# Handing out weight conversions and token sums by summed work, after the attention

## The chip, the core and the metric

The kernel runs on one core of one Trainium2 chip. The metric is the time of one execution on the device, in microseconds (us). A core has TensorE (PE in the rows, with PEld for its weight loads), VectorE (DVE), ScalarE (ACT), GpSimd (POOL) and the DMA queue of SyncE (SP). Each engine works through its own instructions in the order in which the program lists them; an instruction that waits holds up everything behind it on that engine.

## What is computed

An attention with a window of 32 and a few global tokens, over 4 batches, 8 heads and 544 tokens each, then two gated feed-forward blocks over the 2176 tokens that come out of it.

```python
def _attn_ref(q_l, k_l, v_l, q_g, k_g, v_g):
    ...
    mask = np.abs(pos[:, None] - pos[None, :]) <= window
    s_ll = np.where(mask, s_ll, -1000000000.0)
    s_l = np.concatenate([s_lg, s_ll], axis=-1)
    out_l = np.matmul(sm(s_l), np.concatenate([v_g, v_l], axis=2))
    ...
def _moe_ref(x, w_gate, w_val, w_out, rms_g):
    xn = x / rms * rms_g
    g = xn @ w_gate
    return ((g * (1.0 / (1.0 + np.exp(-g)))) * (xn @ w_val) @ w_out)
def _moe2_ref(x, w_gate, w_val, w_out):
    return ((1.0 / (1.0 + np.exp(-(x @ w_gate)))) * (x @ w_val) @ w_out)
```

The model width is 512, the inner width 1536. The weights come in as 64-bit floats and have to be made into 32-bit ones on the chip.

## The kernel before

**Tokens.** The attention works on 16 tiles of 128 local tokens and a 17th tile that holds the global tokens of all batches. Its work is cut into small steps (`st_k`, `st_q`, `st_sg`, `st_a1` and so on), which `slot` lines up in the order of the list `ORDER` (L1070). `st_a1` (L795) writes the window's masks into PSUM by eight small matmuls (L809, 32 rows by 32 columns each) and adds the scores by 64 more (L816). The tokens that come out are held as two 16-bit parts, `xhi` and `xlo`.

**Feed-forward.** The inner width of the two feed-forward stages is cut into 12 blocks g of 256. Blocks 0 to 2 are done plainly: for a unit of up to 384 tokens, `gv_mm` (L303) makes gate and value for j = 0 and j = 1 in 48 matmuls, `gv_post` (L322) puts the gate on (a `t` on ACT and DVE, then `hhi` on ACT and `hlo` on POOL), and `flush` (L1171) sends out the unit before by `out1` (L488, 24 matmuls, which read `hhi` and `hlo`). `flush` stands between j = 0 and j = 1. Blocks 3 to 5 and 7 to 11 are done by `quad_gv` (L385) on a third of the tokens at a time: 84 matmuls (L364) on sums and differences of the weights (`wc`, made from `sm`) and of the tokens (`tt`, made from `xb` or `ya`), which save multiplications. DVE adds up the products from PSUM into `G` and `V` (L421) and multiplies them (L397); ACT and POOL (L401) make `h` from that. PSUM has four pairs for these products. Block 6 is plain again (`plain_gv`), and `out2` writes the sums of the second stage.

**Attention and feed-forward overlap.** `first` (L1097) lists the units of blocks 0 and 1 that are run beside the attention; a unit needs its tokens. `tick` is called after every few matmuls; it runs so many attention steps that the tokens of the coming units are in time (`due`).

**Side work.** Two lists hold work for DVE, ACT and POOL that TensorE doesn't need at once. `w_jobs` has the weight conversions: a DMA into `raw` (three buffers), ACT's scaling of the high word (L139), DVE's shift (L151), sign (L154) and low bits (L157), then the sums `sm` (L249 to L255) and the splitting into `wgv`, `wc` or `wo` (L187 on ACT, L190 on DVE). `jobs` has the token sums: `x_combos` (L616, L590, L596, L599) and, for the second stage, `y_combos` (L627, L630, L590). `tick` (L1116) takes one item of `jobs` every second or third call and one of `w_jobs` every second to fourth (`pace`), whatever DVE has still to do; an item can be as much as three or five DVE instructions. `w_need` and `j_need` run what is left when TensorE comes to need it.

```python
    def tick(n):
        pace[0] += 1
        if jobs and pace[0] % pace[2] == 0:
            i = min(range(len(jobs)), key=lambda i: (jobs[i][0][1], i))
            jobs.pop(i)[1]()
        if pace[0] % pace[1] == 0:
            w_step()
```

Of the kernel before, what the change touches and what calls it, by code (L numbers as in the profile page):

```python
# [1 line left out]

# [17 lines left out]
def tile_attention_moe_moe(  # L20
# [17 lines left out]
    nc = tc.nc  # L38
# [85 lines left out]
    ES = [nc.vector if c == "d" else nc.gpsimd for c in "ppdd"]  # L124
# [20 lines left out]
    def w_bits(n, j, k):  # L145

        u = w_f[n].bitcast(I32)
        js = range(2) if j is None else [j]
        if k == 0:
            v = u if j is None else u[:, j]  # L150
            nc.vector.tensor_scalar(out=v, in0=v, scalar1=3, scalar2=None, op0=ALU.logical_shift_left)  # L151
        for j in js:
            if k == 0:
                nc.vector.scalar_tensor_tensor(out=u[:, j], in0=w_words[n][j][:, :, 1], scalar=-0x80000000, in1=u[:, j],  # L154
                                               op0=ALU.bitwise_and, op1=ALU.bitwise_or)
            else:
                nc.vector.scalar_tensor_tensor(out=u[:, j], in0=w_words[n][j][:, :, 0], scalar=29, in1=u[:, j],  # L157
                                               op0=ALU.logical_shift_right, op1=ALU.bitwise_or)

    def w_conv1(n):  # L160
        w_ahead(2 * n + (3 if wide else 2))
        w_scale(n)
        w_scale(n)
        if wide:
            w_bits(n, None, 0)

    def w_conv2(n):
        if wide:
            w_bits(n, None, 1)
            w_words.pop(n)  # L170
            w_ahead(2 * n + 5)
            w_scale(n + 1)

    def w_half(n, j):
        w_ahead(2 * n + (j + 3 if wide else 2))
        if wide:
            if len(w_words.get(n, [])) <= j:
                w_scale(n)
            w_bits(n, j, 0)
            w_bits(n, j, 1)  # L180
            w_scale(n + j)
            w_ahead(2 * n + j + 4)
            if j == 1:
                w_words.pop(n)

# [7 lines left out]
    w_jobs = []  # L193
    w_late = []
    w_done = {}

    def w_block(g):
# [5 lines left out]
        jobs = []  # L203

        def small(f):

            def f2():
                f()
                w_step()
            return f2  # L210
# [5 lines left out]
        def conv(w):  # L216
            n = 3 * g + w
            if g < GS:
                return [lambda: (late(), w_half(n, 0)), lambda: w_half(n, 1)]
            return [lambda: (late(), w_conv1(n)), lambda: w_conv2(n)]  # L220

        def plain(w, dst):
            def f():
# [4 lines left out]
                w_scale(3 * g + w + 1)  # L228
            return f

        if g < GS:
# [3 lines left out]
            jobs.append(small(alloc))  # L235
            for w in range(2):
                jobs += conv(w) + [plain(w, lambda w=w: [w_t[g][0][:, :, w, a] for a in range(2)])]
        else:
# [3 lines left out]
            jobs.append(small(alloc))  # L242
            box = {}

            def sums(w):
                x = w_f[3 * g + w].rearrange("p j (a f) -> p (j a) f", a=2)
                sm = pb[1].tile([128, 3, 256], F32, tag="sm", name="sm")
                box[w] = x, sm
                ES[0].tensor_tensor(out=sm[:, 0], in0=x[:, 0], in1=x[:, 2], op=ALU.subtract)  # L249
                ES[1].tensor_tensor(out=x[:, 2], in0=x[:, 2], in1=x[:, 3], op=ALU.add)  # L250

            def sums2(w):
                x, sm = box[w]
                ES[2].tensor_tensor(out=sm[:, 1], in0=x[:, 2], in1=x[:, 0], op=ALU.subtract)
                ES[3].tensor_tensor(out=sm[:, 2], in0=x[:, 1], in1=sm[:, 1], op=ALU.subtract)  # L255

# [9 lines left out]
            for w in range(2):  # L266
                jobs += conv(w)
                if g == GP:
                    def parts(w=w):
                        return [w_t[g][0][:, w, a, 0:4].rearrange("p (j a) f -> p j (a f)", j=2) for a in range(2)]  # L270
                    jobs.append(plain(w, parts))
# [992 lines left out]
```

## Time and profile before

| | us |
|---|---|
| median of 3 runs (lowest, highest) | 930.08 (929.59, 931.49) |
| the profiled execution | 930.12 |
| its span, from the first instruction to the last | 928.3 |
| PE busy, of the span | 884.2 (95%) |
| DVE busy | 644.8 (69%) |
| ACT busy | 373.9 (40%) |
| POOL busy | 298.3 (32%) |

The sum is made against the profiled execution: 930.12 us, of which 1.8 us lie outside the span; it is within 0.1 us of the median. Matmuls overlap, so a full PE says only that it had something to do. Where it is not full, or where its granted clock is under 1.00, time is lost that another order may give back. The attention ends near 250 us; blocks 0 to 2 take until 364 us, and what follows belongs to blocks 3 to 11.

### The profile page before, as it was taken

Reading aid. Unit: us, or ns where it says so; the run is one execution under the profiler, and the core shown is the slowest. Engines: PE = TensorE matmul, PEld = TensorE weight load, DVE = VectorE, ACT = ScalarE, POOL = GpSimd, SP = SyncE. Lnnn points to the kernel's source line nnn. Section 1 sums busy time; section 2 is a strip of 40 time slices with the busy share of each in tenths; the row PEclk is TensorE's granted clock in tenths of the full one; section 3 lists DMA queues with packets and bytes.
Section 4 is the critical chain, followed back from the end, with each engine's and each line's share of the span. In section 5 each row is a group of like instructions: output and inputs, shape, how many; then the busy total and the mean of one; then the engine's idle time right before and its main releaser. Section 6 shows DMA issues by size and latency. Waiting matters only on the chain.

```text
span 928.3 us, 19289 instructions
## 1 busy us (share of the span) xinstructions
PE 884.2 (95%) x8119; PEld 549.8 (59%) x8119; DVE 644.8 (69%) x907; ACT 373.9 (40%) x713; POOL 298.3 (32%) x344
## 2 busy tenths in 40 slices
PE   7678889999997999999999799999999999999998
PEld 4556566666674667666666466656556555556553
DVE  2967676446477787899957977738598566997352
ACT  3766666354453342343423444434344223423120
POOL 5544424223256661223221453242122203112120
PEclk9879999999997999999999999999999999999999
DMA  9987874331012111211201211101122011200102
GB/s 193 233 181 153 174 180 99 74 72 25 4 47 90 47 46 46 91 46 46 92 1 46 86 51 46 46 1 47 46 90 92 1 46 46 91 24 1 68 23 102
DMA packets 94183, 67.19 MB, mean 72 GB/s; under 512 B 59280, under 2 KB 84368, under 8 KB 94096
## 3 DMA queue, kind: packets, MB, share of 16 engines
q1 hardware_dynamic: 94096, 65.95, 26.8%
q8 instruction: 64, 1.05, 0.5%
q14 instruction: 23, 0.19, 0.1%
HBM read 52.17 MB, written 4.46 MB: 61 GB/s over the span
## 4 chain that ended last, share of the span: by engine, by line
PE 82%; DVE 10%; issue 3%; ACT 2%; DMA 1%; POOL 1%; SPq 1%; DVEq 0%; POOLq 0%; ACTq 0%
PE p L364 29%; PE p L521 13%; PE b L311 13%; PE p L499 7%; PE b L499 6%; PE p L462 5%; PE b L747 3%; PE b L816 2%; DVE wf L154 2%; PE b L871 2%; DVE wf L157 1%; DVE wf L151 1%; DVE G L421 1%; PE b L789 1%; DMA raw<-in_moe_w_gate_dram 1%
## 5 line engine op out<-in xcount | busy, mean ns | idle before, releaser
L364 PEld LDWEIGHTS <-wc 128*128 128x128 f16 x2016 | 197.4, 98 | 121.1 <-DVE G L421 4.8
L364 PE MATMUL p<-tt,wc 128*128 128x384 f16 (+1 forms) x1152 | 202.0, 319 | 5.9 <-DVE G L421 5.4
L364 PE MATMUL p<-xhi,wc 128*128 128x384 f16 (+1 forms) x576 | 156.3, 317 | 0.0
L401 POOL TENSOR_TENSOR h<-V,h 128x768 f16<-128x768 f32 (+1 forms) x48 | 80.4, 1696 | 235.5 <-ACT h L398 218.3
L311 PE MATMUL b<-xhi,wgv 128*128 128x384 f16 (+1 forms) x576 | 143.0, 319 | 0.0
L521 PE MATMUL p<-wo,h 128*128 128x512 f16 x612 | 133.4, 379 | 0.0
L499 PEld LDWEIGHTS <-wo 128*128 128x128 f16 x864 | 85.2, 99 | 58.4 <-issue 10.9
L311 PEld LDWEIGHTS <-wgv 128*128 128x128 f16 x864 | 83.2, 98 | 45.8 <-issue 1.9
L521 PEld LDWEIGHTS <-h 128*128 128x128 f16 x612 | 59.8, 98 | 71.1 <-POOL h L401 0.2
L311 PE MATMUL b<-xlo,wgv 128*128 128x384 f16 (+1 forms) x288 | 91.6, 318 | 0.4 <-DVE xlo L921 0.4
L364 PE MATMUL p<-xlo,wc 128*128 128x384 f16 (+1 forms) x288 | 91.4, 317 | 0.0
L481 DVE SCALAR_TENSOR_TENSOR ya<-p,ya 128x768 f32<-128x768 f32 (+3 forms) x42 | 42.3, 1017 | 60.6 <-PE p L521 48.2
L499 PE MATMUL b<-hhi,wo 128*128 128x384 f16 (+1 forms) x288 | 76.0, 330 | 7.4 <-ACT hhi L342 4.9
L428 ACT ACTIVATE sa<-p 128x384 f32<-128x384 f32 (+1 forms) x48 | 22.5, 469 | 132.7 <-PE p L364 119.9
L343 POOL TENSOR_TENSOR hlo<-t,hhi 128x384 f16<-128x384 f32 (+1 forms) x36 | 38.5, 1068 | 109.0 <-ACT hhi L342 109.0
L398 ACT ACTIVATE h<-V 128x1536 f16<-128x1536 f32 (+1 forms) x24 | 33.9, 1413 | 93.5 <-DVE V L397 93.5
L499 PE MATMUL p<-h,wo 128*128 128x384 f16 (+1 forms) x432 | 67.3, 317 | 0.0
L421 DVE TENSOR_TENSOR V<-p,V 128x768 f32<-128x768 f32 (+3 forms) x72 | 56.6, 787 | 12.1 <-PE p L364 9.3
L421 DVE TENSOR_TENSOR G<-p,G 128x768 f32<-128x768 f32 (+3 forms) x72 | 56.6, 785 | 8.6 <-PE p L364 6.2
L139 ACT ACTIVATE wf<-raw 128x512 f32<-128x512 f32 x72 | 48.4, 674 | 16.6 <-DMA raw<-in_moe_w_gate_dram 14.3
L157 DVE SCALAR_TENSOR_TENSOR wf<-raw,wf 128x512 int32<-128x512 int32 x72 | 53.8, 779 | 0.6
L154 DVE SCALAR_TENSOR_TENSOR wf<-raw,wf 128x512 int32<-128x512 int32 x72 | 52.4, 758 | 1.6
(137 smaller groups left out, 1296.0 us busy)
## 6 DMA issues: line engine op xcount, KB each, us to landing
raw<-in_moe_w_gate_dram SPq DMA_DIRECT2D x24, 512.0 KB, 4.0
raw<-in_moe_w_val_dram SPq DMA_DIRECT2D x24, 512.0 KB, 4.2
raw<-in_moe_w_out_dram SPq DMA_DIRECT2D x24, 512.0 KB, 3.9
vw<-vt SPq DMA_DIRECT2D x28, 260.0 KB, 5.1
k<-in_k_l_dram SPq DMA_DIRECT2D x16, 256.0 KB, 5.3
q<-in_q_l_dram SPq DMA_DIRECT2D x16, 256.0 KB, 4.5
vt<-in_v_l_dram SPq DMA_DIRECT2D x32, 128.0 KB, 5.0
out_dram<-ya SPq DMA_DIRECT2D x16, 256.0 KB, 2.3
```

Of the source, the lines that this page charges most:

```text
L139: nc.scalar.activation(out=f, in_=words[-1][:, :, 1].bitcast(F32), func=AF.Copy, scale=2.0 ** -112)
L154: nc.vector.scalar_tensor_tensor(out=u[:, j], in0=w_words[n][j][:, :, 1], scalar=-0x80000000, in1=u[:, j], op0=ALU.bitwise_and, op1=ALU.bi ...
L157: nc.vector.scalar_tensor_tensor(out=u[:, j], in0=w_words[n][j][:, :, 0], scalar=29, in1=u[:, j], op0=ALU.logical_shift_right, op1=ALU.bit ...
L311: nc.tensor.matmul(p[:, 0:n], wgv[:, j, gv, a, k * 128:(k + 1) * 128], x[xi][:, k, o:o + n], start=(i == 0), stop=(i == 11),)
L343: EH[3].tensor_tensor(out=lo, in0=t, in1=hi, op=ALU.subtract)
L364: nc.tensor.matmul(p, wc[:, w, a, wi, kt * 128:(kt + 1) * 128], r, start=(i == 0), stop=(i == 5))
L401: EH[j // 2].tensor_tensor(out=lo[:, i:i + 2], in0=vj[:, i - j:i - j + 2], in1=hi[:, i:i + 2], op=ALU.subtract)
L421: nc.vector.tensor_tensor(out=o, in0=p, in1=i, op=ALU.add)
L462: nc.tensor.matmul(gv[:, w], wc[:, w, a, c, (k % 2) * 128:(k % 2 + 1) * 128], x[q][:, k, h * n:(h + 1) * n], start=(i == 0), stop=(i == 11))
L481: nc.vector.scalar_tensor_tensor(out=ya, in0=p, scalar=1.0 / WS, in1=ya, op0=ALU.mult, op1=ALU.add)
L499: nc.tensor.matmul(p[:, i, 0:n], wo[:, j, a, d * 128:(d + 1) * 128], hh[:, j, ho:ho + n], start=(c == 0), stop=(c == 6 * len(gr) - 1),)
L521: nc.tensor.matmul(p[:, i], hh[:, j, (i0 + i) * 128:(i0 + i + 1) * 128], wo[:, j, a, :], start=(c == 0 and g == gr[0]), stop=(c == 5 and g ...
```

## The change

- The weight conversions and token sums are cut into single instructions, each with the letter of its engine (`d`, `a`, `p`). A wrapper around the engines (`Counted`) adds up, in columns of TensorE, the work that has been given to DVE, ACT and POOL, and one more sum for the SBUF port of DVE and POOL.
- Once the attention's steps are all issued, `tick` no longer goes by `pace`: `give` hands out the next instruction only while its engine's sum lies less than `SLACK` = 2400 columns ahead of TensorE's clock, and takes first the list whose due time (`due_w`, `due_j`) is earliest. Up to then `tick` is as it was.
- `flush` moves, after the attention, from between j = 0 and j = 1 to behind the matmuls of j = 1 and ahead of their `gv_post`.
- `first` takes the last four units of block 0 ahead of the last four of block 1, so the attention is asked for its last tokens two units sooner.
- In `ORDER`, `sg` (scores of the global tokens) stands behind `a1` and ahead of `k`.
- The masks are one tile of 5 pieces with 32 zero rows under each 32 rows; the mask matmuls read 64 rows, without `tile_position`, and go through both halves for each of the four column groups. `setup` has 8 selects for them, not 22.

```diff
-    ES = [nc.vector if c == "d" else nc.gpsimd for c in "ppdd"]
+    busy = {"d": 0, "a": 0, "p": 0, "port": 0}
+    clock = [0, 0.0]
...
+                n = int(np.prod(o.shape[1:]))
...
+                sb = all(x == bass.MemoryType.SB for x in ins)
+                one = len(ins) < 2 and sb and self.key == "d"
+                t = max(busy[self.key], clock[0])
+                c = FIX + (self.per / 2 if one else self.per) * n
+                if sb and self.key != "a" and ins:
+                    t = max(t, busy["port"])
+                    busy["port"] = t + c
+                busy[self.key] = t + c
+                return f(*args, **kw)
...
+            self.vector = Counted(nc.vector, "d", 2.45)
+            self.scalar = Counted(nc.scalar, "a", 2.0)
+            self.gpsimd = Counted(nc.gpsimd, "p", 4.5)
...
+        return [(None, start), ("A", lambda: w_scale(n)), ("A", lambda: w_scale(n)),
+                ("d", lambda: w_shift(n, None)), ("d", lambda: w_sign(n, 0)), ("d", lambda: w_sign(n, 1)),
+                ("d", lambda: w_low(n, 0)), ("d", lambda: w_low(n, 1)), (None, end), ("A", lambda: w_scale(n + 1))]
...
+    def due_w():
+        g, i, _ = w_jobs[0]
+        left = sum(len(x[2]) for x in w_jobs if x[:2] == [g, i])
+        return starts.get((g, 0) if i == 0 else (group[g][-1], 1), clock[0]) - STEP * left
...
-    masks = [const.tile([128, 128], BF16, name=f"mask{i}") for i in range(3)]
+    mask = const.tile([128, 5, 32], BF16, name="mask")
...
-                nc.tensor.matmul(two(p[r].rearrange("p r (a c) -> p r a c", c=32)), one[r, r],
-                                 two(mk[r].rearrange("p (a c) -> p a c", c=32)).unsqueeze(1).to_broadcast([32, NPR, 2, 32]),
-                                 start=True, stop=True, tile_position=(32 * i, 32 * i))
+            for e, p in enumerate(ps2):
+                r = slice(64 * e, 64 * e + 64)
+                nc.tensor.matmul(
+                    p[32 * i:32 * i + 32].rearrange("p r (a c) -> p r a c", c=32)[:, :, a:c + 1:c - a],
+                    one[r, 64 * e:64 * e + 32],
+                    mask[r, x:x + 2].unsqueeze(1).to_broadcast([64, NPR, 2, 32]),
+                    start=True, stop=True)
...
-    ORDER = ['g1', 'a1', 'k', 'a2', 'mx', 'sc', 'q', 'g1x', 'sg', 'a3', 'a4', 'ex', 'a4b', 'nm', 'rm', 'g']
+    ORDER = ['g1', 'a1', 'sg', 'k', 'a2', 'mx', 'sc', 'q', 'g1x', 'a3', 'a4', 'ex', 'a4b', 'nm', 'rm', 'g']
...
-    first = [(0, 0, 3), (0, 3, 3), (1, 0, 3), (1, 3, 3), (0, 6, 3), (1, 6, 3), (0, 9, 3), (1, 9, 3), (0, 12, 3), (0, 15, 2), (1, 12, 3), (1, 15, 2)]
+    first = [(0, 0, 3), (0, 3, 3), (1, 0, 3), (1, 3, 3), (0, 6, 3), (0, 9, 3), (0, 12, 3), (0, 15, 2), (1, 6, 3), (1, 9, 3), (1, 12, 3), (1, 15, 2)]
...
+    SLACK = 2400
+    STEP = 2400
...
+    def fits(key, op):
+        if callable(op[0]):
+            return op[0]()
+        e = op[0] and op[0].lower()
+        if e is None:
+            return True
+        if busy[e] > clock[0] + SLACK:
+            return False
+        return op[0] == "A" or ready.get(key, 0) <= max(clock[0], busy[e]) + SLACK
...
     def tick(n):
+        if pos[0] == len(steps):
+            clock[0] += 6 * n
+            give()
+            return
         pace[0] += 1
...
                 gv_mm(g, ch, j, 1)
+                if j == 1 and wi < len(work) - 1:
+                    flush()
                 gv_post(g, ch, j)
                 tick(ch[2])
-                if j == 0 and wi < len(work) - 1:
+                if j == 0 and wi < len(work) - 1 and pos[0] < len(steps):
                     flush()
```

Two places show what that does to the order. In the lists of the changed kernel every vector instruction stands at L67, the line of the wrapper.

DVE, the first place: the last tokens of block 1, soon after the attention; a `t` is what `hhi`, and so the next `out1`, waits for. Before:

```order
L157 SCALAR_TENSOR_TENSOR wf<-raw,wf 128x512
L616 TENSOR_TENSOR xb<-xhi_73,xlo_76 128x768
L590 TENSOR_TENSOR xb<-xb 128x768
L190 SCALAR_TENSOR_TENSOR wgv<-wf,wgv 128x2x512
L151 TENSOR_SCALAR wf<-wf 128x512
L154 SCALAR_TENSOR_TENSOR wf<-raw,wf 128x512
L157 SCALAR_TENSOR_TENSOR wf<-raw,wf 128x512
L590 TENSOR_TENSOR xb<-xb 128x384
L151 TENSOR_SCALAR wf<-wf 128x512
L154 SCALAR_TENSOR_TENSOR wf<-raw,wf 128x512
L157 SCALAR_TENSOR_TENSOR wf<-raw,wf 128x512
L334 SCALAR_TENSOR_TENSOR t<-b,t 128x384
```

The same tokens of block 1 in the changed kernel:

```order
L67 SCALAR_TENSOR_TENSOR t<-b,t 128x384
L67 TENSOR_TENSOR xb<-xb 128x384
L67 SCALAR_TENSOR_TENSOR t<-b,t 128x256
L67 SCALAR_TENSOR_TENSOR ya_81<-b,ya_81 128x384 x2
L67 TENSOR_TENSOR xb<-xhi_74,xlo_77 128x768
L67 SCALAR_TENSOR_TENSOR ya_81<-b,ya_81 128x384 x2
L67 TENSOR_TENSOR xb<-xb 128x768
L67 SCALAR_TENSOR_TENSOR t<-b,t 128x256
L67 TENSOR_TENSOR xb<-xb 128x384
L67 SCALAR_TENSOR_TENSOR t<-b,t 128x384
```

Ahead of that last `t` stand thirteen conversions and token sums since the `t` before (eleven of them are shown); in the changed kernel two `t` have one or two token sums and some accumulations of `out1` between them, and block 2's conversions stand earlier.

DVE, the second place: block 5's last third of the tokens, the `G` half of its products. Before:

```order
L397 SCALAR_TENSOR_TENSOR V<-V,G 128x1536
L421 TENSOR_TENSOR G<-p,sa 128x2x320
L590 TENSOR_TENSOR ya_79<-ya_79 128x768
L157 SCALAR_TENSOR_TENSOR wf<-raw,wf 128x512 x2
L421 TENSOR_TENSOR G<-p,G 128x2x320
L421 TENSOR_TENSOR G<-p,G 128x320
L590 TENSOR_TENSOR ya_79<-ya_79 128x384
L421 TENSOR_TENSOR G<-p,G 128x2x320
L421 TENSOR_TENSOR V<-p,sa 128x2x320
L190 SCALAR_TENSOR_TENSOR wc<-wf,wc 128x1024
L151 TENSOR_SCALAR wf<-wf 128x1024
L154 SCALAR_TENSOR_TENSOR wf<-raw,wf 128x512 x2
```

The same third in the changed kernel:

```order
L67 SCALAR_TENSOR_TENSOR V<-V,G 128x1536
L67 TENSOR_TENSOR G<-p,sa 128x2x320
L67 SCALAR_TENSOR_TENSOR wf<-raw,wf 128x512
L67 TENSOR_TENSOR G<-p,G 128x2x320
L67 TENSOR_TENSOR G<-p,G 128x320
L67 TENSOR_TENSOR G<-p,G 128x2x320
L67 TENSOR_TENSOR V<-p,sa 128x2x320
L67 TENSOR_TENSOR xlo_76<-ya_79,xhi_73 128x768
L67 TENSOR_TENSOR V<-p,V 128x2x320
L67 TENSOR_TENSOR V<-p,V 128x320
L67 TENSOR_TENSOR V<-p,V 128x2x320
L67 SCALAR_TENSOR_TENSOR V<-V,G 128x4x320
```

Of eight conversions and sums two are left in that third; the others have moved into the long stretches of `out1` before it and `plain_gv` behind it.

## Rows read from the trace of the kernel before

**Rows 1.** The page: span, and the granted clock in 40 slices (tenths).

```profile
span 928.3 us, 19289 instructions
PEclk9879999999997999999999999999999999999999
```

**Rows 2.** Stretches: length, busy us (xinstructions) by engine, granted clock, DMA share, GB/s.

```profile
70.00:98.20 28.20, 22.92 (x515) 16.59 (x517) 20.29 (x43) 18.72 (x60) 12.06 (x25) 0.94 0.82 167
98.20:130.40 32.20, 28.05 (x539) 18.42 (x538) 22.34 (x41) 20.30 (x53) 9.61 (x17) 1.00 0.73 170
130.40:277.00 146.60, 146.60 (x2082) 99.19 (x2082) 81.86 (x164) 73.42 (x193) 53.62 (x80) 1.00 0.27 61
277.00:300.00 23.00, 17.10 (x93) 10.26 (x92) 18.95 (x26) 8.92 (x15) 12.77 (x10) 0.79 0.28 91
500.00:525.00 25.00, 19.98 (x128) 12.81 (x126) 23.34 (x26) 12.24 (x15) 8.02 (x5) 0.93 0.26 85
525.00:850.00 325.00, 324.12 (x1942) 189.41 (x1941) 242.96 (x295) 121.95 (x158) 88.81 (x66) 1.00 0.14 48
```

**Rows 3.** Timeline, 268 to 281 us: start, duration, instruction, idle time before it.

```profile
268.27 0.56 DVE L334 SCALAR_TENSOR_TENSOR t<-b,t 128x384 f32<-128x384 f32 x1 [1.34 <-PE b L311]
...
279.69 0.55 DVE L334 SCALAR_TENSOR_TENSOR t<-b,t 128x384 f32<-128x384 f32 x1
...
280.85 0.48 PE L499 MATMUL b<-hhi,wo 128*128 128x384 f16 x1 [3.06 <-ACT hhi L342]
```

**Rows 4.** Timeline, 513 to 520 us.

```profile
513.01 0.95 DVE L590 TENSOR_TENSOR ya<-ya 128x768 f32<-128x768 f32 x1
...
513.73 3.77 POOL L401 TENSOR_TENSOR h<-V,h 128x768 f16<-128x768 f32 x2 [8.84 <-ACT h L398]
513.87 4.17 DVE L157 SCALAR_TENSOR_TENSOR wf<-raw,wf 128x512 int32<-128x512 int32 x2
...
517.97 1.33 DVE L421 TENSOR_TENSOR G<-p,G 128x640 f32<-128x640 f32 x2
...
519.36 0.98 PE L364 MATMUL p<-tt,wc 128*128 128x320 f16 x3 [4.43 <-DVE G L421]
```

**Rows 5.** DVE from 262 us on, by line and shape: count | busy us, mean ns.

```profile
L157 DVE SCALAR_TENSOR_TENSOR wf<-raw,wf 128x512 int32<-128x512 int32 x60 | 43.8, 766 | 0.2
L154 DVE SCALAR_TENSOR_TENSOR wf<-raw,wf 128x512 int32<-128x512 int32 x60 | 43.2, 756 | 1.1
...
L190 DVE SCALAR_TENSOR_TENSOR wc<-wf,wc 128x1024 f16<-128x1024 f32 x18 | 23.9, 1326 | 6.6 <-ACT wc L187 6.6
L151 DVE TENSOR_SCALAR wf<-wf 128x1024 int32<-128x1024 int32 x27 | 23.7, 879 | 0.0
...
L481 DVE SCALAR_TENSOR_TENSOR ya<-b,ya 128x384 f32<-128x384 f32 x24 | 12.2, 548 | 2.2 <-PE b L499 2.1
...
L630 DVE TENSOR_TENSOR xlo<-ya,xhi 128x768 f16<-128x768 f32 x4 | 6.0, 1492 | 0.0
L616 DVE TENSOR_TENSOR xb<-xhi,xlo 128x768 f32<-128x768 f16 x3 | 5.6, 1873 | 0.6 <-POOL tt L599 0.6
...
L590 DVE TENSOR_TENSOR ya<-ya 128x768 f32<-128x768 f32 x4 | 4.5, 1116 | 0.0
...
L590 DVE TENSOR_TENSOR xb<-xb 128x768 f32<-128x768 f32 x3 | 2.9, 950 | 0.1
L590 DVE TENSOR_TENSOR ya<-ya 128x384 f32<-128x384 f32 x4 | 2.5, 635 | 0.0
```

**Rows 6.** Chain of waits, 395 to 435 us: start, us, what.

```profile
398.69 11.41 PE p L364 x84
410.10 7.80 PE p L499 x48
```

**Rows 7.** Timeline of PE, 110.5 to 113 us: masks and scores of one token tile.

```profile
110.84 0.40 PE L809 MATMUL b<-mask,ident 32*32 32x256 bf16 x8
111.17 1.16 PE L816 MATMUL b<-kT,qT 64*32 64x128 f32 x64
```

More of the change, by code (lines that the diff above doesn't have):

```diff
@@ L143, in w_ahead, with w_shift @@
             w_load()
-    def w_bits(n, j, k):
+    def w_shift(n, j):
         u = w_f[n].bitcast(I32)
[L148 to L158, printed above, removed]
@@ new lines, in w_block, with due_j @@
+        i0 = next(i for i, x in enumerate(groups) if m in x)
+        for i, x in enumerate(groups):
+            w_jobs.append([g, int(i > i0), x])
+    starts = {}
+    def due_w():
+        g, i, _ = w_jobs[0]
+        left = sum(len(x[2]) for x in w_jobs if x[:2] == [g, i])
+        return starts.get((g, 0) if i == 0 else (group[g][-1], 1), clock[0]) - STEP * left
+    def due_j(key):
+        q, k = key
+        left = sum(len(x[1]) for x in jobs if x[0] == key)
+        if k == 0:
+            t = starts[GP, q]
+        else:
+            t = min(t for (g, p), t in starts.items() if p == q and g not in (2, GP) and t > clock[0])
+        return t - STEP * left
@@ L1110, in tile_attention_moe_moe, with plan_starts, run_op, give @@
     work += [(g, ch, None) for g in range(2, GS) for ch in chunks_b]
-    clock = [0, 0.0]
     pace = [0, 2, 2]
+    ready = {}
+    SLACK = 2400
+    STEP = 2400
+    def plan_starts(todo):
+        t = clock[0]
+        pend = None
+        for g, q, n, c in todo:
+            starts.setdefault((g, q), t)
+            t += c * n
+            if pend:
+                t += pend
+            pend = 24 * n if g < GS else 48 * n * len(group[g]) if g == group[g][-1] else None
+    def fits(key, op):
[7 more added lines that the diff above has]
+        return op[0] == "A" or ready.get(key, 0) <= max(clock[0], busy[e]) + SLACK
+    def run_op(key, op):
+        e, f = op
+        if isinstance(e, str):
+            k = e.lower()
+            if e != "A":
+                busy[k] = max(busy[k], ready.get(key, 0))
+            f()
+            ready[key] = busy[k]
+        else:
+            f()
+    def give():
+        while True:
+            c = []
+            if w_jobs:
+                c.append((due_w(), "w", w_jobs, 0))
+            for k in range(2):
+                i = [i for i, x in enumerate(jobs) if x[0][1] == k]
+                if i:
+                    key = jobs[i[0]][0]
+                    if k == 0 or not any(x[0] == (key[0], 0) for x in jobs):
+                        c.append((due_j(key), key, jobs, i[0]))
+            for _, key, js, i in sorted(c, key=lambda x: x[0]):
+                g = js[i][2] if key == "w" else js[i][1]
+                if fits(key, g[0]):
+                    run_op(key, g.pop(0))
+                    if not g:
+                        js.pop(i)
+                    break
+            else:
+                return
     def tick(n):
+        if pos[0] == len(steps):
+            clock[0] += 6 * n
+            give()
+            return
         pace[0] += 1
```

210 lines of the change are left out of this document (127 added, 83 removed).

## The prediction

> **What bounds the kernel now.** I read the stretches first, because busy shares of the whole span hide where TensorE (PE) has nothing to do. PE is full from 130 to 277 us, and after 300 us in all but two places [rows 2]. So this kernel ends when PE has streamed its matmuls, and only three kinds of time can be won: idle PE, PE at the lower of its two clock levels (1.2 instead of 2.4 GHz), and PE work that is removed. The clock line falls under nine tenths in three of 40 slices of 23.2 us: the second and third, and the thirteenth, from 278 to 301 us [rows 1].
>
> After the attention there are two holes. From 277 to 300 us PE is busy 17.10 of 23 us at a mean granted clock of 0.79; from 500 to 525 us 19.98 of 25 at 0.93; from 525 to 850 us only 0.88 us are missing [rows 2]. The timeline shows why. In the first, the `t` that `out1` waits for starts at 279.69 although the one ahead of it started at 268.27: 11.42 us between two of them, DVE working through conversions and token sums, and PE stands 3.06 us until `hhi` is there [rows 3]. In the second, DVE does a token sum and two low-bit instructions, which take 4.17 us instead of two times 0.766, while POOL makes `h`; the addition that frees PSUM starts at 517.97 and PE has stood 4.43 us [rows 4, 5]. Both are the same thing: side work is handed to DVE by a count of ticks, and sits in front of what PE waits for. DVE is not full on the whole (242.96 of 325 us later on [rows 2]).
>
> **The change part by part, against the profiled execution's 930.12 us (0.04 above the median).**
>
> *Handing out by sums, and the later `flush`.* First hole: 23 − 17.10 = 5.90 us idle. A mean clock of 0.79 over 23 us costs at most 0.21 × 23 = 4.8 us more, and less by what fell on idle time; spread evenly it is 0.21 × 17.10 = 3.6. Together 9.5 (5.9 to 10.7). Second hole: 25 − 19.98 = 5.02 us idle, and 0.07 × 19.98 = 1.4 for the clock: 6.4 (5.0 to 6.8). With the 0.88 us from 525 to 850 us that is 16.8 us, at least 11.8 and at most 18.4 [rows 2].
>
> What of it comes back? In the first place the order now has no more than two token sums between two `t`, with four accumulations: 1.873 + 0.950 + 4 × 0.548 = 5.0 us [rows 5] instead of 11.42 [rows 3]. Also `out1` now reads what was made a whole unit's 48 matmuls earlier: 48 matmuls of 384 columns take 7.80 us [rows 6], where before it was the 24 of one j, 3.9 us. The hole should close. In the second place the third of block 5 loses 1.116 + 2 × 0.766 + 0.635 + 1.326 + 0.879 + 2 × 0.756 = 7.0 us of DVE work and gets 0.766 + 1.492 = 2.3 [rows 5]: 4.7 us less beside matmuls that take 11.41 [rows 6], against a stand of 5.02. That closes it nearly. What is moved lands beside `out1` and `plain_gv`, where DVE has little to do. What hides it there is PE's own length: if a conversion ran late, `w_need` would put the rest in front of the block, and PE would wait for it. New waits: the four accumulations now stand ahead of the `t` of j = 1, and ACT and POOL wait for that `t`; its two PSUM banks are held for the 24 matmuls of `out1`, 3.9 us longer, and asked for again after another unit's j = 0, 3.9 us later. That fits. The DMAs go with the conversions: each conversion now asks for its next `raw` when it ends, and ACT's scaling can stand behind that transfer. I leave 1.5 us for all such small waits (0 to 6.8, the second hole over again). Gain: 16.8 − 1.5 = 15.3.
>
> A piece of that can fail. The trace shows the low-bit instruction at 4.17 / 2 = 2.1 us beside POOL's `h`, against a mean of 0.766 [rows 4, 5]. The Trainium skill has a rule for it (GPSIMD Engine Reference, 8. Key points): GpSimd shares its SBUF interfaces with VectorE and contends with VectorE instructions that have two SBUF inputs. The trace agrees, since `raw` and `wf` both lie in SBUF. It speaks against handing DVE conversions while POOL works, and the change only counts that port in a sum; what it would give is the second rival below.
>
> *Masks over 64 rows.* The eight masks take 0.33 us from their first to the first score, and the 64 scores that follow, which have the form that the masks now get, 1.16 us, 18 ns each, as many run side by side [rows 7]. No row has the new form. Bounds: nothing saved, or all 0.33 us, 16 times 5.3 us. That it costs time I exclude, because the scores show eight such products side by side. I take half, 0.17 us, and only for the some nine tiles that meet a full PE: 1.5 us. Fourteen selects fewer in `setup` run on POOL in the first microseconds and free nothing that PE waits for: nothing.
>
> The Trainium skill has a rule here too (TensorEngine Tiling (Array Packing), Key Properties): changing the tiling mode drains TensorE. By it the whole 0.33 us less one round of masks would go, some 0.2 us a tile as an estimate, and the sum would be 0.3 us lower. No row separates the drain.
>
> *The order of units, and `sg`.* No work is removed. Two units fewer run beside the attention: 72 matmuls each, 7.80 × 1.5 = 11.7 us [rows 6], so 23.4 us of cover move from the attention to behind it. The cover is not lost, it is done later. What it hid: from 130 to 277 us DVE is busy 56% and ACT 50% [rows 2]; in 123 us it would be 67% and 60%. That is no bound by sums, but waits in single steps get less cover. From 98 to 130 us, with DVE at 69% and ACT at 63%, PE lost 4.15 us of 32.2 [rows 2]. I add 2 us (from −2, if this hole shrinks, to 8, the 13% of that stretch on some 65 more microseconds). `sg` ahead of `k` delays one set of transposes by 16 small matmuls and their two copies; I take nothing, within these bounds.
>
> **Sum.** 930.12 − 15.3 − 1.5 + 2.0 = 915.3 us.
>
> **The rivals.**
>
> *The attention gets tighter than I think.* Less cover, and every tile loses some 1.2 us at waits for ACT and DVE: 8 us rather than 2, 921.3, and with half of the first hole kept 925. For it: 98 to 130 us. Against it: the full PE from 130 on with 44% of DVE free.
>
> *The port moves the stand elsewhere.* The sums close one place, but conversions still run beside POOL's `h` at 2.1 us, and two stands like that of the second hole, 4.43 us each [rows 4], come up at other blocks: 915.3 + 8.9 = 924. Against it: where a third of a block has only one such instruction, it costs 1.4 us, which four PSUM pairs can hide.
>
> *Slower.* The attention breaks up: with less cover PE stands so often that the clock goes down, as from 70 to 98 us, where PE was busy 22.92 of 28.20 us (81%) at 0.94 [rows 2]. If the 115 us or so from 98 us to the attention's end went so, it would cost 115 × (0.19 + 0.81 × 0.06) = 27 us: 915.3 − 2 + 27 = 940. It decides from the point where a tile's longest path through ACT and DVE exceeds its matmuls and cover; before, 130 to 277 us, it didn't.
>
> *The change doesn't do what it says.* The sums run off from the real engines, conversions come as late as before: 930.1 − 1.5 = 928.6.
>
> *Better.* Everything comes back, 18.4 us, the masks 3.0 and 4.15 in the attention: 930.1 − 25.5 = 904.6.
>
> **How the numbers follow.** The forecast has 0.57 with its own range of 909 to 920; the tight attention 0.18, the port 0.10, slower 0.07, no effect 0.03, better 0.05. The range of 905 to 925 takes in the forecast, most of the tight attention and the port, and leaves out slower, no effect and the rest. A measurement tells 0.2%, 1.9 us, from no change. Faster than 928.2: 0.90; slower by more than that: 0.07; between: 0.03.
>
> **What would show it.** In the changed profile PE should be full between 277 and 300 us and where block 5 ends, and the clock 1.00 from the attention's end to the last matmul; if DVE still releases PE there, the handing out failed. The attention should end by some 20 us sooner, with at most 6 us of PE idle between 98 us and its end; more than 10 is the first rival. Masks to scores should read 0.1 to 0.2 us. Low bits at 2 us with PE idle behind them would be the port. I would be wrong altogether if the two holes were not waits for DVE's order but for DMAs.

## The result, and the profile after

The changed kernel takes 916.81 us (median of four runs, 916.03 to 919.95), against 929.84 us for the kernel before beside it; the ratio is 0.9865 (95% interval 0.9837 to 0.9892). The profiled execution took 916.03 us at a span of 913.9 us, 14.4 us less than the span of before [rows 1]. The forecast of 915.3 us is 1.5 us below the median, and the range of 905 to 925 us holds it.

The page of the changed kernel, the span and the granted clock of TensorE (PE) in 40 slices of 22.8 us. The dent in the thirteenth slice of before [rows 1] is gone; the early ones, now in the second to fourth slice, are not:

```profile
span 913.9 us, 19244 instructions
...
PEclk9868999999999999999999999999999999999999
```

Stretches of the kernel after, with the columns of [rows 2] (length, busy us of PE, its weight loads, DVE, ACT and POOL, granted clock, DMA share, GB/s):

```profile
70.00:98.20 28.20, 23.76 (x541) 17.80 (x534) 19.61 (x39) 18.66 (x59) 11.34 (x23) 0.92 0.82 172
98.20:130.40 32.20, 27.48 (x599) 18.59 (x597) 24.02 (x49) 19.68 (x57) 12.03 (x21) 1.00 0.71 159
130.40:277.00 146.60, 146.60 (x2025) 99.66 (x2024) 90.01 (x171) 78.85 (x200) 59.16 (x83) 1.00 0.35 79
277.00:300.00 23.00, 23.00 (x162) 15.60 (x160) 12.88 (x24) 7.71 (x15) 17.10 (x13) 1.00 0.00 1
500.00:525.00 25.00, 25.00 (x165) 15.94 (x163) 19.52 (x23) 10.28 (x14) 13.83 (x9) 1.00 0.07 22
...
575.00:600.00 25.00, 22.86 (x133) 12.61 (x131) 18.38 (x23) 11.20 (x15) 11.99 (x9) 1.00 0.14 43
...
252.00:900.00 648.00, 645.42 (x3976) 388.36 (x3975) 473.46 (x594) 224.91 (x304) 186.67 (x142) 1.00 0.16 50
```

Both holes of before [rows 2] are closed: PE is full from 277 to 300 us and from 500 to 525 us, at a clock of 1.00. From 252 to 900 us, behind the attention in both kernels, PE is idle 648 − 645.42 = 2.58 us; before it was 648 − 636.19 = 11.81 us, with the clock below 1.00 on top. Nearly all that is left is one new place, from 575 to 600 us: 2.14 us. From 252 to 900 us the kernel before reads:

```profile
252.00:900.00 648.00, 636.19 (x3930) 385.70 (x3929) 485.48 (x595) 234.25 (x318) 198.85 (x146) 0.99 0.15 49
```

The attention ends with its last `xlo`, which begins at 229.94 us instead of 252.86, 22.9 us sooner. In the kernel before, and then in the kernel after (shortest, median and longest in ns, then the first and the last start, from 60 us on):

```profile
L921 DVE TENSOR_TENSOR xlo<-b,xhi x15: 673/691/693, 69.9 to 252.9; 128x512 f16<-128x512 f32 x15
```

```profile
L67 DVE TENSOR_TENSOR xlo<-b,xhi x16: 672/692/693, 60.3 to 229.9; 128x512 f16<-128x512 f32 x16
```

The timeline of the kernel after at the two old places, answering [rows 3, 4]: start, duration, instruction, and in brackets the idle time before it and what ended it.

```profile
257.99 0.55 DVE L67 SCALAR_TENSOR_TENSOR t<-b,t 128x384 f32<-128x384 f32 x1
...
266.12 0.55 DVE L67 SCALAR_TENSOR_TENSOR t<-b,t 128x384 f32<-128x384 f32 x1
...
268.82 0.56 DVE L67 SCALAR_TENSOR_TENSOR t<-b,t 128x384 f32<-128x384 f32 x1
...
277.74 0.55 DVE L67 SCALAR_TENSOR_TENSOR t<-b,t 128x384 f32<-128x384 f32 x1
...
520.14 2.73 DVE L67 SCALAR_TENSOR_TENSOR wf<-raw,wf 128x512 int32<-128x512 int32 x2
520.14 4.23 POOL L67 TENSOR_TENSOR tt<-ya,tt 128x768 f16<-128x768 f32 x2
...
523.16 0.96 DVE L67 SCALAR_TENSOR_TENSOR ya<-p,ya 128x768 f32<-128x768 f32 x1 [0.29 <-PE p L574]
```

In the first place the `t` of j = 1 still comes 8.1 and 8.9 us behind that of j = 0. In the first pair seven conversions and four accumulations stand between them, in the second two token sums and four accumulations, and DVE itself waits there for what PE makes; but PE works on in the meantime and waits for none of it. In the second the low bits still meet POOL (2.73 us for two that take 0.69 each alone), but they now run beside `out1` of blocks 4 and 5 (L574), and what follows them on DVE, the accumulation at 523.16, waits for PE and not the other way round.

The new place, in the timeline of the kernel after:

```profile
584.84 2.45 DVE L67 SCALAR_TENSOR_TENSOR V<-V,G 128x1536 f32<-128x1536 f32 x1
...
587.32 1.48 ACT L67 ACTIVATE h<-V 128x1536 f16<-128x1536 f32 x1 [3.37 <-DVE V L67]
...
588.88 3.24 POOL L67 TENSOR_TENSOR h<-V,h 128x768 f16<-128x768 f32 x2 [3.21 <-ACT h L67]
...
590.58 0.82 PE L596 MATMUL p<-wo,h 128*128 128x512 f16 x3 [1.33 <-POOL h L67]
...
592.17 2.12 PE L596 MATMUL p<-wo,h 128*128 128x512 f16 x9 [0.78 <-POOL h L67]
```

It is the first `out2` of the second stage, written into `plain_gv` for q = 2 behind its j = 0. It needs `h` of the quad just before it: product on DVE (2.45 us, beside POOL's `tt`, where the mean of this form is 1.80), copy on ACT, difference on POOL in two halves. PE reaches it after 48 matmuls of 320 columns (6.5 us) and waits 1.33 and 0.78 us.

The masks, answering [rows 7], for the tile at the same place:

```profile
110.15 0.30 PE L890 MATMUL b<-mask,ident 64*32 64x256 bf16 x8
110.27 1.13 PE L899 MATMUL b<-kT,qT 64*32 64x128 f32 x64
```

From the first mask to the first score it is 0.12 us instead of 0.33. The other tiles from 98 us on read the same, 0.12 against 0.32 or 0.33.

### The profile page after: what moved, and what is told of

The parts are those of the page before. It is cut to its first block, busy times and chain, and to the rows that moved or that the text cites. A ratio compares the mean times of both kernels' runs of the same rounds, so it can differ in the third digit from the quotient of the medians.

```text
span 913.9 us, 19244 instructions
## 1 busy us (share of the span) xinstructions
PE 878.7 (96%) x8119; PEld 550.4 (60%) x8119; DVE 634.4 (69%) x903; ACT 372.1 (41%) x713; POOL 291.7 (32%) x328
## 4 chain that ended last, share of the span: by engine, by line
PE 80%; DVE 11%; ACT 3%; issue 2%; SPq 1%; DMA 1%; POOL 1%; ACTq 0%; DVEq 0%; POOLq 0%
PE p L439 31%; PE p L596 14%; PE b L386 14%; PE b L574 7%; PE p L574 6%; DVE wf L67 3%; PE b L831 3%; PE b L954 2%; PE b L899 1%; DVE V L67 1%; PE p L537 1%; DVE G L67 1%; ACT h L67 1%; DVE ya L67 1%; PE b L873 1%
## 5 line engine op out<-in xcount | busy, mean ns | idle before, releaser
L67 POOL TENSOR_TENSOR h<-V,h 128x768 f16<-128x768 f32 (+1 forms) x48 | 76.7, 1618 | 280.7 <-ACT h L67 260.5
L67 DVE SCALAR_TENSOR_TENSOR wf<-raw,wf 128x512 int32<-128x512 int32 x144 | 113.1, 811 | 2.0
L574 PEld LDWEIGHTS <-wo 128*128 128x128 f16 x864 | 84.3, 98 | 46.9 <-issue 0.3
L67 DVE SCALAR_TENSOR_TENSOR ya<-p,ya 128x768 f32<-128x768 f32 (+3 forms) x42 | 42.3, 1017 | 57.2 <-PE p L596 42.8
L67 ACT ACTIVATE h<-V 128x1536 f16<-128x1536 f32 (+3 forms) x30 | 36.9, 1231 | 105.9 <-DVE V L67 105.9
L574 PE MATMUL b<-hhi,wo 128*128 128x384 f16 (+1 forms) x288 | 71.1, 317 | 0.4 <-ACT ya L67 0.4
L67 POOL TENSOR_TENSOR hlo<-t,hhi 128x384 f16<-128x384 f32 (+1 forms) x36 | 35.1, 974 | 101.7 <-ACT hhi L67 101.7
L574 PE MATMUL p<-h,wo 128*128 128x384 f16 (+1 forms) x432 | 67.3, 317 | 0.0
L67 ACT ACTIVATE sa<-p 128x384 f32<-128x384 f32 (+1 forms) x48 | 22.5, 468 | 101.8 <-PE p L439 89.3
L67 DVE TENSOR_TENSOR V<-p,V 128x768 f32<-128x768 f32 (+3 forms) x72 | 56.5, 785 | 8.9 <-PE p L439 7.0
L67 DVE TENSOR_TENSOR G<-p,G 128x768 f32<-128x768 f32 (+3 forms) x72 | 56.5, 785 | 6.8 <-PE p L439 4.6
L67 ACT ACTIVATE wf<-raw 128x512 f32<-128x512 f32 x72 | 48.5, 673 | 16.8 <-DMA raw<-in_moe_w_gate_dram 14.0
L67 POOL COPY vw<-vt 32x520 f32<-32x520 f32 (+1 forms) x64 | 47.1, 736 | 13.5 <-DMA vt<-in_v_l_dram 10.6
```

The source lines that it names most:

```text
L67: return f(*args, **kw)
L574: nc.tensor.matmul(p[:, i, 0:n], wo[:, j, a, d * 128:(d + 1) * 128], hh[:, j, ho:ho + n], start=(c == 0), stop=(c == 6 * len(gr) - 1),)
```

## The experiments

Each is the kernel after with the edit shown, unless another is named. Median and ratio are both given, since each was timed beside its own runs of the kernel before.

### Both halves of the handing out undone

```diff
     def tick(n):
-        if pos[0] == len(steps):
-            clock[0] += 6 * n
-            give()
-            return
         pace[0] += 1
...
-                if j == 1 and wi < len(work) - 1:
-                    flush()
                 gv_post(g, ch, j)
                 tick(ch[2])
-                if j == 0 and wi < len(work) - 1 and pos[0] < len(steps):
+                if j == 0 and wi < len(work) - 1:
                     flush()
```

> The kernel after, with conversions and token sums handed out by counts of ticks again and `flush` at its old place throughout; masks, `sg` and the order of units stay new. Theory A, the prediction's: both holes come back, 14 to 16.8 us less what the new small waits cost: 916.8 + 14.2 (17.6 us short of full speed after the attention before, 3.4 us now) = 931. Theory B: the new order of units alone moves the conversions away from the attention's end, and only the second hole (5.0 to 6.8 us) comes back: 920 to 924. Theory C: handing out matters little: 917 to 918.

Measured: 931.77 us, ratio 1.0011 (0.9997 to 1.0026). Stretches of this kernel:

```profile
252.00:277.00 25.00, 18.55 (x107) 10.42 (x106) 21.61 (x29) 10.76 (x18) 11.87 (x9) 0.95 0.28 85
...
500.00:525.00 25.00, 19.97 (x123) 12.62 (x122) 23.35 (x26) 12.05 (x15) 9.00 (x5) 0.86 0.25 85
```

Both holes are back, the first some 23 us earlier, since the attention now ends that much sooner. Theory A, within 1 us: with masks, `sg` and order of units new and the handing out old, nothing of the gain is left.

### One half at a time

The handing out undone, `flush` left new (the first half of the diff above):

> The kernel after, with only the handing out undone (side work by counts of ticks again); `flush` stays behind j = 1. With both undone it measured 931.8. Theory A: the handing out does it all, and this reads 930 to 932. Theory B: the later `flush` closes the first hole alone (3.9 us more for `hhi`, against 7.1 us short of full speed at 250 to 275 us with both undone), and the second stays (7.6 us short): 923 to 925.

Measured: 929.99 us, ratio 0.9992 (0.9979 to 1.0005). Stretches of this kernel:

```profile
252.00:277.00 25.00, 20.89 (x127) 12.20 (x125) 21.20 (x27) 10.79 (x21) 10.87 (x7) 1.00 0.32 102
...
500.00:525.00 25.00, 19.97 (x128) 12.76 (x127) 23.46 (x26) 10.67 (x14) 9.02 (x5) 0.93 0.21 71
```

`flush` undone, the handing out left new (the second half):

> The kernel after, with only `flush` back at its old place (behind j = 0 throughout, so that `out1` reads an `hlo` made 24 matmuls earlier). Theory A: the handing out by sums closes both holes, and the later `flush` hides nothing that is still there: 916.8 to 918. Theory B: the first hole, where TensorE waited for `hhi` in `out1`, needs the later `flush` as well, since 24 matmuls of 384 columns are 3.9 us only: waits of 1 to 3 us at several units, 919 to 923.

Measured: 920.89 us, ratio 0.9885 (0.9860 to 0.9910). What PE waits for in this kernel from 252 to 900 us (total us, times, longest):

```profile
PE p L596 <- POOL h L67: 2.1, 2, 1.3
PE b L574 <- POOL hlo L67: 2.1, 3, 0.8
PE b L574 <- ACT hhi L67: 1.3, 2, 0.9
```

The first of these rows is the place that the kernel after has too; the other two, 3.4 us, are `out1` waiting for `hhi` and `hlo` that were made only 24 matmuls earlier: 1.8 us of it from 252 to 300 us, 1.6 from 325 to 350. So the handing out does nearly all (13 us of the 15 by medians), the second hole hangs on it alone, and the later `flush` takes the last 2 to 4 us out of the plain blocks (4.1 us by medians, 1.9 by ratios, whose intervals overlap). Theory A for the one, theory B for the other.

### The order of units undone

```diff
-    first = [..., (1, 3, 3), (0, 6, 3), (0, 9, 3), (0, 12, 3), (0, 15, 2), (1, 6, 3), (1, 9, 3), (1, 12, 3), (1, 15, 2)]
+    first = [..., (1, 3, 3), (0, 6, 3), (1, 6, 3), (0, 9, 3), (1, 9, 3), (0, 12, 3), (0, 15, 2), (1, 12, 3), (1, 15, 2)]
```

> The kernel after, with the old order of units (two more units beside the attention). Theory A, the prediction's: less cover made the attention tighter by 2 us, so with the old order it ends some 23 us later and the whole is 2 us shorter: 914.8. Theory B, from the traces: TensorE was idle 4.72 us from 98 to 130 us and nowhere after, against 4.15 before, so the cover is worth 0.6 us at most: 916.2 to 916.8. Theory C: the old order of units is what piled up the conversions, and part of the first hole (up to 9.5 us) comes back behind the attention: 919 to 926.

Measured: 925.42 us, ratio 0.9945 (0.9928 to 0.9963): 8.6 us slower than the kernel after, where the prediction had the old order 2 us better. Two stretches of this kernel:

```profile
98.20:130.40 32.20, 29.48 (x589) 20.32 (x590) 24.32 (x47) 21.65 (x58) 10.92 (x20) 1.00 0.82 176
...
350.00:375.00 25.00, 17.85 (x103) 10.70 (x103) 14.54 (x24) 6.24 (x8) 9.83 (x9) 0.86 0.12 42
```

The 2 us are there: in the attention PE is idle 32.20 − 29.48 = 2.72 us instead of 4.72. But from 350 to 375 us it loses 7.15 us, and the clock falls to 0.86. The timeline of this place:

```profile
352.80 0.83 DVE L67 TENSOR_TENSOR xb<-xhi,xlo 128x640 f32<-128x640 f16 x1 [3.94 <-POOL tt L67]
352.85 2.03 POOL L67 TENSOR_TENSOR xb<-xhi,xlo 128x640 f32<-128x640 f16 x1
...
356.18 3.26 DVE L67 SCALAR_TENSOR_TENSOR ya<-b,ya 128x384 f32<-128x384 f32 x8
...
359.49 0.48 PE L439 MATMUL p<-xhi,wc 128*128 128x384 f16 x1 [7.04 <-DVE ya L67]
```

These are the token sums of the last tokens (`xb`, then `tt`), written by `j_need` in front of the quads because they had found no room before. They go back and forth between DVE, POOL and ACT; behind them on DVE stand eight accumulations that free PSUM, and PE stands 7.04 us. In the kernel after nothing is left for `j_need` there: the last `tt` starts at 340.97 us, and the quads start at 353.12. 23 us more of PE work lie between the attention's end and this point, and the sums fit in beside it. That is what the new order of units gives.

### The order of units undone, and the forced sums out of the way

```diff
+        flush()
         for q in range(3):
             j_need(q, 1)
-        flush()
         st_p0.close()
```

together with the old order of units.

> The kernel after, with the old order of units (that alone measured 925.4, with one stand of 7.04 us at 352 us, where token sums that had found no room are forced out by DVE and POOL ahead of the accumulations that free PSUM), and with these forced sums written behind the last `out1` of the plain blocks instead of ahead of it. Theory A: the stand is the forced sums, and the order of units is worth only the room that it leaves for them: 925.4 - 7 to 9 = 916 to 918; if less cover had made the attention tighter by 2 us, as predicted, 915. Theory B: the sums are then in the way of the first quads, whose additions free PSUM too, and most stays lost: 921 to 925.

Measured: 918.51 us, ratio 0.9860 (0.9846 to 0.9874), 6.9 us faster than without the two lines. PE from 98.2 to 130.4 us is busy 29.61 us, and from 252 to 900 us:

```profile
252.00:900.00 648.00, 641.54 (x3975) 388.20 (x3974) 479.75 (x598) 232.31 (x317) 197.79 (x147) 1.00 0.16 51
```

That is nearest to theory A, half a microsecond above its range: the stand was the forced sums and not the order as such. The attention costs 2.1 us less than in the kernel after (2.59 us idle against 4.72), the stretch behind it 3.9 us more (6.46 against 2.58), so the old order repaired is about as fast as the new one, by another road.

### The new wait taken away: the fastest version

```diff
-                if j == 0 and h == 1:
+                if (j, h) == ((1, 0) if q == 2 else (0, 1)):
                     flush()
```

> The kernel after, with one block's `flush` later: in `plain_gv` for q = 2 the `out2` that waits for POOL's `h` (2.1 us of idle TensorE at 590 us, 2.6 us short of full speed, and 4.3 to 4.5 in two of the runs, where the clock also fell) comes 48 matmuls of 320 columns later. Theory A: these 6.5 us hide the wait: 916.8 - 2.1 to 4.5 = 912.5 to 914.7. Theory B: the wait moves, since the `out2` then holds PSUM pairs and POOL against the quads that follow: 916 to 917.5.

Measured: 912.76 us (910.5 to 914.5), ratio 0.9797 (0.9779 to 0.9815), faster than both kernels. Stretch and timeline of this kernel:

```profile
252.00:900.00 648.00, 647.55 (x3991) 389.93 (x3989) 473.65 (x595) 224.95 (x305) 186.53 (x142) 1.00 0.16 50
```

```profile
589.36 3.25 POOL L67 TENSOR_TENSOR h<-V,h 128x768 f16<-128x768 f32 x2 [3.21 <-ACT h L67]
...
591.24 9.01 PE L596 MATMUL p<-wo,h 128*128 128x512 f16 x41
```

POOL's `h` is as late as in the kernel after (589.36 us), but `out2` comes at 591.24 and runs through. Between (0, 1) and (1, 0) lie 24 matmuls, 3.3 us, and not the 48 of the expectation; they suffice. Theory A. The idle time fell by 2.13 us and the time of the profiled execution by 2.20, from 916.03 to 913.83; the median fell by 4.1, and by ratios it is 6.3. What makes the rest is not shown. It may be the clock, which in some executions goes down at this stand, as in the profiles of the kernel after with the old masks and with the old `sg` (below), where 575 to 600 us has 0.93.

### The masks undone

`st_a1` and `setup` as before: eight masks of 32 rows, three mask tiles. First on the kernel after, then on the fastest version.

> The kernel after, with the masks of before (32 rows each, three mask tiles). Theory A: every one of the 16 tiles then has 0.21 us more TensorE work from first mask to first score (0.33 us instead of 0.12), and all of it lies on the path: 916.8 + 3.3 = 920.1. Theory B, the prediction's: only the nine tiles that meet a full TensorE pay, 918.3 to 918.7. Theory C: the early attention waits for other engines anyway and the rest hides too: 916.8 to 917.3.

> The kernel with the later `out2` (the run that measured 912.8 and has no stand left behind the attention above 0.2 us), with the masks of before. This separates the masks from the stand at 590 us, which came out 1.7 to 2 us longer by chance in the profile of the earlier masks run. Theory A, the prediction's: 0.17 to 0.21 us for each of some nine tiles: 912.8 + 1.5 to 1.9 = 914.3 to 914.7. Theory B: nothing, since the attention ended at 230.1 us with the old masks and between 229.7 and 230.3 with the new ones in five profiles: 912.8 within 1 us, and the attention's end at 230 again. Theory C: all 16 tiles, 916.1.

Measured: 917.99 us, ratio 0.9865 (0.9844 to 0.9886), against 916.81 and 0.9865; and 914.81 us, ratio 0.9820 (0.9796 to 0.9844), against 912.76 and 0.9797. That is +1.2 and +2.1 us by medians, 0 and +2.1 by ratios, and the intervals overlap in both pairs. The profile of the first was 2.3 us longer than that of the kernel after, but some 1.6 of these us (an estimate, 0.07 × 22.81) lie at 575 to 600 us, where the clock was 0.93 and no mask runs. The last `xlo` begins at 230.4 and 231.0 us, against 229.8 to 230.5 in six profiles with the new masks and the new order (the times of the attention in the expectations are some 0.25 us lower throughout). The theory that all 16 tiles pay, 3.3 us, falls, since it would have moved that end by as much; between the prediction's 1.5 us and nothing the runs do not decide.

### `sg` undone

```diff
-    ORDER = ['g1', 'a1', 'sg', 'k', 'a2', 'mx', 'sc', 'q', 'g1x', 'a3', ...]
+    ORDER = ['g1', 'a1', 'k', 'a2', 'mx', 'sc', 'q', 'g1x', 'sg', 'a3', ...]
```

> The kernel after, with `sg` back at its old place (behind `g1x`, ahead of `a3`). Theory A, from the two traces: the new place costs the early attention something, since `xlo` of the first four tiles is written 1.5 to 2.2 us later than before (45.9, 60.1, 71.8, 81.3 us against 44.0, 58.2, 69.6, 79.8) and TensorE then runs at the lower clock level for 30.7 us of the first 130 instead of 23.9. Undone, it gives 1.5 to 2 us: 914.8 to 915.3 against 916.8. Theory B, the prediction's: the place is worth nothing, 916.8 within 1 us, and the late tiles come from something else. Theory C: the new place helps the later tiles, and without it the attention ends later: 918 to 919.

> The kernel with the later `out2` (912.8), with `sg` at its old place. Theory A: the place is worth 3 us to the attention, which ended at 232.9 us with `sg` at the old place and at 229.7 to 230.3 with the new: 915.8. Theory B, the prediction's: nothing, and the 3.2 us were one execution's lower clock: 912.8 within 1 us, the attention's end at 230 to 231.

Measured: 918.15 us, ratio 0.9868 (0.9847 to 0.9888); and on the fastest version 915.95 us, ratio 0.9831 (0.9809 to 0.9852). By medians +1.3 and +3.2 us, by ratios +0.3 and +3.2, and again the intervals overlap in both pairs. The stretch in which the two places differ, in the first of these kernels and in the second:

```profile
98.20:130.40 32.20, 26.70 (x535) 18.16 (x528) 22.10 (x44) 17.96 (x52) 10.45 (x19) 0.95 0.66 142
```

```profile
98.20:130.40 32.20, 27.00 (x543) 18.53 (x528) 22.18 (x41) 17.82 (x52) 10.35 (x18) 0.89 0.64 147
```

With `sg` at the old place the first three tiles are ready 1 to 4 us sooner, and from 98 to 130 us PE is idle 0.8 us more than in the kernel that each is compared with (5.50 against 4.72, 5.20 against 4.36) and has a lower clock. The whole time came out between 0.3 and 3.2 us against the old place; nothing bears out my theory that the new place costs 2 us, and how much it gains, if anything, stays open.

### One unit more beside the attention

```diff
-    ... (0, 6, 3), (0, 9, 3), (0, 12, 3), (0, 15, 2), (1, 6, 3), (1, 9, 3), ...
+    ... (0, 6, 3), (1, 6, 3), (0, 9, 3), (0, 12, 3), (0, 15, 2), (1, 9, 3), ...
```

on the fastest version.

> The kernel with the later `out2` (912.8), with one unit more beside the attention (block 1's third unit ahead of block 0's fourth) and so 11.7 us of matmuls less behind it. Theory A: the attention gains half of the 2.1 us that the old order gave it (TensorE idle 2.6 to 2.7 us from 98 to 130 us instead of 4.7), and the room left behind it still holds the token sums: 911.5 to 912. Theory B: the sums find too little room again, and a part of the 7 us stand at the end of the plain blocks returns: 914 to 918. Theory C: the cover has to be there at 98 to 130 us, where this order changes nothing: 912.8.

Measured: 913.07 us, ratio 0.9805 (0.9775 to 0.9836), no difference from 912.76. The stretch of the attention in this kernel, and one behind it:

```profile
98.20:130.40 32.20, 29.89 (x657) 20.66 (x660) 25.43 (x50) 22.95 (x63) 13.81 (x23) 1.00 0.83 183
...
325.00:350.00 25.00, 23.09 (x150) 14.77 (x148) 16.82 (x26) 9.61 (x18) 14.07 (x13) 0.95 0.13 43
```

PE is idle 2.31 us there, against 4.36 in the fastest version, so this one unit is worth all of the 2 us that the attention can gain. Behind it, from 325 to 350 us, 1.91 us are idle at a clock of 0.95 (`out1` waits for `hhi` and `hlo`), and the two cancel.

### The port not counted

```diff
                 if sb and self.key != "a" and ins:
-                    t = max(t, busy["port"])
                     busy["port"] = t + c
```

on the fastest version; the two engines' own sums stay.

> The kernel with the later `out2` (912.8), whose planner no longer counts the port that VectorE and GpSimd share (their sums stay). Theory A, the prediction's second rival: instructions with two SBUF inputs then meet POOL's more often and take 2.1 us instead of 0.77; one or two stands of 2 to 4.4 us come back: 915 to 921. Theory B: the two engines' own sums keep the order right, 912 to 914, and the port is not what the gain hangs on.

Measured: 955.93 us, ratio 1.0266 (1.0240 to 1.0291): 43 us slower than the version it was made from, and 25 us slower than the kernel before. Neither theory had that. From 252 to 900 us PE is idle 34.79 us, in pieces at more than ten places:

```profile
252.00:900.00 648.00, 613.21 (x3747) 366.56 (x3746) 463.10 (x575) 218.45 (x297) 184.82 (x138) 0.99 0.15 48
```

One of them in the timeline of this kernel:

```profile
577.25 3.56 POOL L66 TENSOR_TENSOR tt<-ya,tt 128x768 f16<-128x768 f32 x2
...
577.49 1.82 DVE L66 TENSOR_TENSOR h<-G,h 128x384 f16<-128x384 f32 x1 [0.59 <-ACT h L66]
...
579.23 2.13 DVE L66 TENSOR_SCALAR wf<-wf 128x1024 int32<-128x1024 int32 x1
...
581.40 1.90 DVE L66 SCALAR_TENSOR_TENSOR wf<-raw,wf 128x512 int32<-128x512 int32 x3
...
583.21 0.55 DVE L66 SCALAR_TENSOR_TENSOR V<-p,V 128x384 f32<-128x384 f32 x1
...
583.81 0.32 PE L536 MATMUL p<-xhi,wc 128*128 128x384 f16 x1 [1.68 <-DVE V L66]
```

DVE does a difference and a shift stretched beside POOL's `tt`, then three low-bit instructions, and only then the product that frees PSUM. With the port in the sum, the work of both engines on SBUF is laid end to end, and so handed out no faster than one after the other would take; without it, both get their share at once. Whether the loss is the stretching or simply that side work comes too fast is not separated here; a smaller `SLACK` without the port would be the test, and it was not run. For the second: the mean of the sign and low-bit instructions from 230 to 900 us is 0.809 us in this kernel and 0.808 in the kernel after, so these are not longer. The shifts are (0.867 against 0.775 us for the 27 of 128x1024, 0.785 against 0.465 for the 6 of 128x512), which makes 4.4 us, far less than the 34.79 lost. That speaks for side work at the wrong places, without proving it.

## Why the prediction came out as it did

**The two holes, 16.8 us.** Right in place, cause and size. The forecast of 15.3 left 1.5 us for new small waits; in the profile 2.58 us are left, nearly all of it one wait of 2.1 us for POOL's `h`, and the clock stays at 1.00, so 14.2 us of the 16.8 came back. One row of the working was off: no more than two token sums and 5.0 us of work between two `t`. The trace has 8.1 and 8.9 us, and seven conversions in one of the pairs. The hole closes all the same, since `out1` then reads what was made a unit earlier; with `flush` at its old place it waits again, 3.4 us. The new wait is of the kind that the prediction named (an engine that is late where PE gets to its block), but it looked for it at w_need and ACT, not at `out2` of the second stage. Taken away, it gave 4.1 us.

**What closes them.** The first hole was put down to the handing out and the later `flush` together, the second to the handing out. The two halves confirm it: without the handing out 929.99, without the later `flush` 920.89, with neither 931.77. Of the parts of the handing out only the port's sum was tried alone; single instructions, the 2400 columns and the due times were not.

**The order of units, +2.0 us.** Here a step failed, though its number was right. The attention does pay 2.0 to 2.1 us for the smaller cover (4.72 us idle against 2.72 and 2.59), from 98 to 130 us, the stretch from which the prediction took its bound. Six profiles with the new order and masks and the new `sg` have 4.33 to 4.87 us there; the kernel before, with all three old, has 4.15. What the prediction left out is what follows from its own sentence, "The cover is not lost, it is done later." Later it covers the token sums. Without that room they are forced out at the end of the plain blocks, and PE stands 7.04 us there with the clock down: in all the old order is 8.6 us slower. The gain that the prediction booked under the handing out needs the order of units, or the forced sums out of the way, as well. That its sum came out right without this is luck: for the old order the same sum, without the 2.0, gives 913.3 us, and the run took 925.42. In the kernel before, token sums were handed out by counts, whether PE waited behind them or not, so its trace did not show that they need room.

**Masks, −1.5 us, and `sg`, nothing.** From 0.33 to 0.12 us from masks to scores, within the 0.1 to 0.2 forecast; on the whole time 0 to 2.1 us, which holds the 1.5 without proving it. (Eight tiles of before begin from 98 us on and six from 130, where PE is full; the prediction took some nine.) The 0.21 us saved a tile is the 0.2 us that the prediction had worked out by the Trainium skill (TensorEngine Tiling (Array Packing), Key Properties: changing the tiling mode drains TensorE), and more than the half of 0.33 that it took itself. No run separates the drain from the smaller number of rounds. `sg` was put at nothing; the runs read 0.3 to 3.2 us gained, with intervals that overlap.

**The port.** As a rival it did not happen: no stand of 4.43 us came up at another block, but the new wait at 590 us has a DVE product of 2.45 instead of 1.76 us at its head. But "the change only counts that port in a sum" was far too light: taking it out of the sum costs 43 us.

**The other rivals.** The tight attention: 4.72 us idle from 98 to 130 us and nothing after, below the 6 us allowed. (With half of the first hole's 9.5 us kept this rival comes to 926 us, not 925.) Slower by the clock: the clock is 1.00 from 98 us on. (From there to the attention's end it is 132 us, not 115, which would have made this rival 945 us.) No effect: both holes are closed. The attention's end came 22.9 us sooner, as forecast.

The remaining 0.2 us of the 14.4 in the span (14.2 behind the attention, of which the part for the clock is an estimate) is what masks, order of units, `sg` and the early clock leave together; the prediction had +0.5 us for the first three.

## What to carry to other kernels

Side work has two needs: it must not stand in front of what the bound engine waits for, and it must have enough of that engine's work beside it before it is due; a change of order that looks like a loss of cover can be what makes room for the second. When a planner replaces counts, look at what its "needed by now" clause still forces out, and at the first consumer behind each forced piece. A shared resource in a planner's sums can act as the brake that keeps the whole order right, so take it out in an experiment before calling it a detail.

## What the runs showed of the hardware

VectorE instructions whose operands all lie in SBUF were held up beside GpSimd instructions, also the shift with its single input; those that read PSUM were not. The shift `wf<-wf` of 128x1024 takes 0.69 us alone and up to 2.13 us beside POOL's `tt` (the row at 579.23 above); the low-bit instruction likewise 0.69 and up to 2.13, and a product of 128x1536 1.76 and 2.45. The accumulation `ya<-p,ya`, which reads PSUM, took its usual 0.96 us at 523.16 in the kernel after, while POOL made `tt`, and none of that kernel's 72 additions `V<-p,V` (two of them at 581.26 us, beside POOL's `ya`) took more than 0.96. GpSimd loses as well: two `tt` from 520.14 on take 4.23 us there, where two `h` of the same size take 3.24. The Trainium skill says that the pair of ports which the two share is locked for a whole instruction and the loser blocks (SBUF — State Buffer, Terms). These rows fit that: an instruction of 0.69 us reaches 2.13, and 1.44 us is less than the 1.62 us of one such POOL instruction. No run here tests it further.

At the stand of about 2 us near 590 us the clock went down in some executions and not in others. From 575 to 600 us the granted clock was 1.00 in the profiles of the kernel after, of `flush` undone and of the forced sums moved, with 2.09 to 2.18 us of idle PE; it was 0.93 in those of the old masks and the old `sg`, with 2.19 and 2.32 us. The last two, masks first:

```profile
575.00:600.00 25.00, 22.81 (x125) 12.25 (x124) 18.87 (x23) 11.11 (x15) 9.78 (x7) 0.93 0.13 43
```

```profile
575.00:600.00 25.00, 22.68 (x128) 12.66 (x127) 20.96 (x26) 9.75 (x14) 8.68 (x6) 0.93 0.14 43
```
